# Convolution and two feed-forward layers on one core: early products issued singly, filler on TensorE, x split in thirds, a PSUM tile per bank

## The chip, the core and the metric

The kernel runs on one core of a Trainium2 chip. The time is the device time of one execution, in microseconds (us). A core has TensorE (PE; its weight loads are PEld), VectorE (DVE), ScalarE (ACT), GpSimd (POOL), and SyncE (SP), which issues the DMAs here. Every engine works through its own instructions in the order in which the program lists them.

## The reference

x is (2, 4096, 192), the convolution's weights (2, 4096, 8 heads, 7 taps); both layers have 2048 inner columns.

```python
w = softmax(weight_gen)                          # over the 7 taps
out = einsum('bshk,bskhg->bshg', w, x_unfolded)  # causal, 24 columns per head
x = out.reshape(8192, 192)
h = maximum(x @ w_in, 0.0);  y = h * h @ w_out                     # layer m=0
h = y @ w_in2;  z = (h * clip(h + 3, 0, 6) / 6) @ w_out2           # layer m=1
```

## The kernel before

The 8192 tokens are 16 blocks b of 512 columns. Each layer m takes a block in 8 steps, (m, b, f); a step covers two groups (FG) of 128 inner columns. All float32 operands of a product are split into a high and a low part in a reduced format, so a step has three sets of products: high by high, low weight by high, high by low.

A step has a part A (`make_A`, line 307: 18 matmuls of 64 rows into h, two at a time on the two halves of the array; group i uses rows 64i and up, so the 192 rows of x stand twice, once in each half) and a part B (`make_B`, line 318: the squared or gated h times w_out, into the sums `accs`, 128 rows and 64 rows). `emit_pair` (line 350) interleaves part A of one step with part B of the step three before (LAG = 3), the latter cut into 20 products of 64 rows; where there is no part A, as in the last three steps, part B is 10 products of 128 rows, first the six of the 128 rows (o = 0), then the four of the 64 rows (o = 1, line 361). Between A and B stand `relu` (ScalarE, line 386), `square` (ScalarE, 390) or `gate` (VectorE, 399), `high` (a cast, either engine, 406) and `low` (VectorE, 412). The tiles g, gh and gl have two buffers each.

The first two blocks (b < ON_PE = 2) have a start of their own. `convolve_pe` (line 671): VectorE multiplies one tap (`term`), TensorE adds it up in PSUM with an identity as weights (`total`, line 690: 4 matmuls of 64 rows per tap). `twice` (line 241) copies each third of the sums doubled into `x`, `turn_pe` (line 249) transposes it into `xt`, `split_pe_hi` (261) and `split_pe_lo` (266) split it, two thirds at once and then the last. Later blocks are convolved on VectorE alone (lines 642, 656) and transposed by VectorE and a round over DRAM; `split_hi` (228) and `split_lo` (234) split those. The sixteen steps of blocks 0 and 1 are woven, so that two steps in a row use one group of weights. The weights come as float64 words and are split by VectorE and ScalarE (lines 118 to 176), eight groups for each layer.

All operations are entered with a duration for each engine, what they depend on and which buffers they take; a list scheduler then plays them through and lists the instructions in the order of its start times. On each engine it takes, of what can start, the operation whose time limit is nearest. `finish_last` (line 471) brings out the last block: two evictions (488 on ScalarE, 490 on VectorE), eight small products (498, 499), two copies and two DMAs (504).

## Time and profile before

| | us |
|---|---|
| median of 3 runs | 1104.89 (1103.47 to 1105.0) |
| the profiled execution | 1104.57 |
| its span, first to last instruction | 1102.7 |
| TensorE busy | 1081.8 (98%) |
| VectorE busy | 929.1 (84%) |
| ScalarE busy | 597.4 (54%) |

Busy shares are means over the whole span. TensorE's matmuls are pipelined, so a busy TensorE is not yet at its peak, and its clock has two levels, 1.2 and 2.4 GHz; the page gives the granted clock as a share of the full one. What bounds a stretch is read from tables by stretch and from the chain of waits, which follows the work that ended last back to what released it.

### The profile page before, as it was taken

To read this page: it belongs to the slowest core of one execution; us is meant where nothing else is said; L and a number is where in the kernel's file an instruction comes from. 1 tells how busy PE (TensorE), PEld (TensorE's weight loads), DVE (VectorE), ACT (ScalarE), POOL (GpSimd) and SP (SyncE) were. 2 spreads that over 40 slices of the span, in tenths; PEclk is the share of its full clock that TensorE was granted. 3 is DMA by queue.
4 is the path that set the end of the run, shared out by engine and by line. 5 is a ranking of instruction groups with operands and counts; after the bars stand their busy time and mean duration, and the time that the engine had idled before them with its cause. 6 is when DMAs were issued, how large, how long until landed. Compare 5 with 4: busy or idle time off the path is not lost.

```text
span 1102.7 us, 23858 instructions
## 1 busy us (share of the span) xinstructions
PE 1081.8 (98%) x9846; PEld 934.3 (85%) x9846; DVE 929.1 (84%) x1018; ACT 597.4 (54%) x648; POOL 3.2 (0%) x11
## 2 busy tenths in 40 slices
PE   6899999999999999999999999999999999999998
PEld 3588888888888888888888888888888888888886
DVE  7799999999999999988787576676757888888875
ACT  3799999766645656363553536444353333333322
POOL 1000000000000000000000000000000000000000
PEclk9999999999999999999999999999999999999999
DMA  9702744043330622332221222212032222133101
GB/s 217 186 1 73 198 120 151 20 117 87 78 116 15 175 58 78 97 87 59 61 75 36 62 59 73 58 39 73 21 82 59 68 64 73 45 81 83 30 30 43
DMA packets 67509, 86.73 MB, mean 79 GB/s; under 512 B 5517, under 2 KB 43533, under 8 KB 66505
## 3 DMA queue, kind: packets, MB, share of 16 engines
q1 hardware_dynamic: 67256, 85.01, 29.3%
q8 instruction: 77, 1.26, 0.5%
q14 instruction: 32, 0.25, 0.1%
q10 hardware_dynamic: 144, 0.20, 0.0%
HBM read 59.10 MB, written 26.08 MB: 77 GB/s over the span
## 4 chain that ended last, share of the span: by engine, by line
PE 93%; DVE 3%; DMA 1%; ACT 1%; issue 1%; SPq 0%; DVEq 0%
PE acc L304 48%; PE h L304 44%; DMA st<-in_moe_w_in_dram 1%; PE acc L690 1%; DVE gl L412 1%; DVE a L656 0%; ACT g L386 0%; DMA xc<-in_x_dram 0%; ACT gh L406 0%; PE acc L361 0%; DVE g L399 0%; DVE sl L266 0%; DVE w L164 0%; SPq L90 0%; ACT x L247 0%
## 5 line engine op out<-in xcount | busy, mean ns | idle before, releaser
L304 PE MATMUL h<-sh,w 64*128 64x512 f32 x3072 | 524.6, 378 | 8.2 <-DVE sl L266 6.8
L304 PE MATMUL acc<-gh,w 64*128 64x512 f32 x3036 | 517.9, 376 | 0.0
L386 ACT ACTIVATE g<-h 128x1024 f32<-128x1024 f32 x256 | 262.2, 1024 | 469.4 <-PE h L304 448.2
L304 PEld LDWEIGHTS h<-sh,w 64*128 64x128 f32 x3072 | 383.3, 186 | 51.5 <-DVE sl L266 7.2
L304 PEld LDWEIGHTS acc<-gh,w 64*128 64x128 f32 x3036 | 379.8, 186 | 40.2
L304 PE MATMUL h<-sl,w 64*128 64x512 f32 x1536 | 358.7, 378 | 0.0
L304 PE MATMUL acc<-gl,w 64*128 64x512 f32 x2024 | 354.1, 376 | 0.0
L412 DVE TENSOR_TENSOR gl<-g,gh 128x1024 fp32r<-128x1024 f32 x256 | 312.3, 1220 | 15.9 <-ACT gh L406 11.3
L304 PEld LDWEIGHTS acc<-gl,w 64*128 64x128 f32 x2024 | 237.8, 186 | 26.8
L304 PEld LDWEIGHTS h<-sl,w 64*128 64x128 f32 x1536 | 238.7, 187 | 20.7
L399 DVE SCALAR_TENSOR_TENSOR g<-g,h 128x1024 f32<-128x1024 f32 x128 | 156.0, 1219 | 60.5 <-ACT g L386 59.7
L406 DVE CAST gh<-g 128x1024 fp32r<-128x1024 f32 x156 | 107.1, 686 | 44.9 <-PE acc L304 43.8
L390 ACT ACTIVATE g<-g 128x1024 f32<-128x1024 f32 x128 | 135.8, 1061 | 1.3
L406 ACT CAST gh<-g 128x1024 fp32r<-128x1024 f32 x100 | 104.4, 1044 | 4.2 <-PE acc L361 1.3
L642 DVE TENSOR_TENSOR pr<-xc,wc 128x768 f32<-128x768 f32 x84 | 79.8, 952 | 1.3 <-DMA xs<-aT 0.6
L656 DVE TENSOR_TENSOR a<-a,pr 128x768 f32<-128x768 f32 x84 | 79.7, 949 | 0.0
L234 DVE TENSOR_TENSOR sl<-x,sh 128x1536 fp32r<-128x1536 f32 x30 | 52.5, 1749 | 3.7 <-ACT sh L228 3.7
L424 DVE TENSOR_SCALAR z<-acc 128x512 f32<-128x512 f32 x30 | 20.7, 690 | 24.6 <-PE h L304 24.5
L228 ACT CAST sh<-x 128x1536 fp32r<-128x1536 f32 x27 | 39.8, 1474 | 1.6 <-DMA x<-xs 1.5
L690 PE MATMUL acc<-pp,ident 64*64 64x384 f32 x112 | 21.8, 548 | 6.6 <-DVE pp L681 6.6
L690 PEld LDWEIGHTS acc<-pp,ident 64*64 64x64 f32 x112 | 8.9, 152 | 18.5 <-issue 17.9
L128 ACT COPY t<-st 128x768 uint16<-128x768 uint16 x16 | 19.2, 1202 | 7.7 <-DMA st<-in_moe_w_out_dram 6.8
(54 smaller groups left out, 276.9 us busy)
## 6 DMA issues: line engine op xcount, KB each, us to landing
x<-ys SPq DMA_DIRECT2D x32, 512.0 KB, 6.2
x<-xs SPq DMA_DIRECT2D x28, 384.0 KB, 5.1
xc<-in_x_dram SPq DMA_DIRECT2D x7, 1344.0 KB, 7.5
ys<-z SPq DMA_DIRECT2D x32, 256.0 KB, 2.0
st<-in_moe_w_in_dram SPq DMA_DIRECT2D x32, 192.0 KB, 6.4
zq<-zs SPq DMA_DIRECT2D x60, 96.0 KB, 2.3
out_dram<-o SPq DMA_DIRECT2D x15, 384.0 KB, 2.3
xs<-aT SPq DMA_DIRECT2D x56, 96.0 KB, 2.9
```

The source lines that it names most:

```text
L228: copy_on(engine)(xs_in[m, b][0], xraw[m, b][:, 0:NK])
L234: nc.vector.tensor_tensor(out=lo, in0=src, in1=hi.bitcast(F32), op=ALU.subtract)
L304: return lambda: nc.tensor.matmul(ps, w[r], turns(x[r]), start=start, stop=stop)
L386: nc.scalar.activation(g, ps, AF.Relu, bias=3.0 if m else 0.0)
L390: nc.scalar.activation(g, g, AF.Square)
L399: nc.vector.scalar_tensor_tensor(out=g, in0=g, scalar=6.0, in1=h_ps[m, b, f], op0=ALU.min, op1=ALU.mult)
L406: copy_on(engine)(gh, g)
L412: nc.vector.tensor_tensor(out=gl, in0=g, in1=gh.bitcast(F32), op=ALU.subtract)
L424: nc.vector.tensor_scalar(out=dst, in0=src, scalar1=scale, scalar2=None, op0=ALU.mult)
L642: nc.vector.tensor_tensor(out=dst, in0=xs, in1=ws.to_broadcast([P, TB, H, G]), op=ALU.mult)
L656: nc.vector.tensor_tensor(out=total(), in0=total(), in1=prods.pop((b, k)), op=ALU.add)
L690: nc.tensor.matmul(attn[b][r, a, 0:2 * D], ident[r, r], v[r, a * 2 * D:(a + 1) * 2 * D], start=k == K - 1, stop=k == 0,)
```

## The change

Six things change. (1) For the first 16 steps part A and part B are separate operations: `products` is called once for A and, for the step's own part B, once more; part B alone is the form with 10 products of 128 rows. From step 16 on they are interleaved as before. (2) `spin` puts products identity x identity into PSUM columns that nobody reads, where the scheduler's TensorE has a gap of more than 0.8 us before 45 us; the first time it plans 4.2 us, then the gap less 0.4. (3) The sums have a PSUM tile for each bank (`acc_tiles`) instead of one for two banks; the taps are added by matmuls of 128 rows. (4) The first two blocks' x is copied once plus its first 64 columns (`copy_sums`), transposed in three overlapping windows, two of them into the sums' own tiles, and split third by third; in part A the second half of the array takes the thirds in another order (`by`). (5) The last step's part B begins with the 64 rows; `finish_last` evicts the 128 rows in two halves on two engines, and gh, gl of the step before the last get buffers of the split x. (6) The scheduler: a tap's sum is entered with 1.3 instead of 0.75 us, the first loads earlier, and an engine may hold back an operation for one that is more urgent by over GAIN = 6 us and would come before it ends less HOLD = 0.8. `relu` loses an argument and `relu_square`, which nothing called, goes; ON_PE is now TURNED.

```diff
-    def twice(b, j, engine):
-        if j == 0:
-            xraw[0, b] = x_tile()
-        d = xraw[0, b][:, j].rearrange("p (t h r) -> p t h r", t=TB, h=2)
-        src = attn[b][:, :, 0:2 * D].rearrange("p a (t d) -> p a t d", t=2)[:, :, :, j * HP:(j + 1) * HP]
-        for a in range(2):
-            copy_on(engine)(d[:, 2 * a:2 * a + 2], src[:, a].unsqueeze(2).to_broadcast([P, 2, 2, HP]))
+    xps, plain, spare, adding = {}, {}, [], []
+    def copy_sums(b, a, engine):
+        if a == 0:
+            plain[b] = x_tile().rearrange("p k n -> p (k n)")[:, 0:TB * (D + HP)].rearrange("p (t d) -> p t d", t=TB)
+        dst = plain[b][:, 2 * a:2 * a + 2]
+        src = attn[b][a][:, 0:2 * D].rearrange("p (t d) -> p t d", t=2)
+        copy_on(engine)(dst[:, :, 0:D], src)
+        copy_on(engine)(dst[:, :, D:], src[:, :, 0:HP])
 
     def turn_pe(b, j):
-        if j % 2 == 0:
-            xps[b, j] = ps_h.tile([P, 2, N], F32, tag="h", name="xt")
-        d = xraw[0, b][:, j].rearrange("p (t c) -> p t c", t=TB)
-        pv = xps[b, j // 2 * 2][:, j % 2].rearrange("d (q t r) -> d t q r", q=Q, t=TB)
+        if j < 2:
+            xps[b, j] = attn[b][j]
+        else:
+            room = ps_h.tile([P, 2, N], F32, tag="h", name="xt")
+            xps[b, j] = room[:, 0]
+            spare.append(room[:, 1, 0:P])
+        pv = xps[b, j].rearrange("d (q t r) -> d t q r", q=Q, t=TB)
         for t in range(TB):
-            nc.tensor.transpose(pv[:, t], d[:, t], ident)
+            nc.tensor.transpose(pv[:, t], plain[b][:, t, j * HP:j * HP + P], ident)
 
     def split_pe_hi(b, j, engine):
         if j == 0:
             xs_in[0, b] = [split_tile(n) for n in "hl"]
-        n = min(2, NK - j)
-        copy_on(engine)(xs_in[0, b][0][:, j:j + n], xps[b, j][:, 0:n])
+        copy_on(engine)(xs_in[0, b][0][:, j], xps[b, j])
 
     def split_pe_lo(b, j):
-        n = min(2, NK - j)
-        hi, lo = [v[:, j:j + n] for v in xs_in[0, b]]
-        nc.vector.tensor_tensor(out=lo, in0=xps[b, j][:, 0:n], in1=hi.bitcast(F32), op=ALU.subtract)
+        hi, lo = [v[:, j] for v in xs_in[0, b]]
+        nc.vector.tensor_tensor(out=lo, in0=xps[b, j], in1=hi.bitcast(F32), op=ALU.subtract)
...
     def make_A(m, b, f):
         w = [[w_in_of(m, f, h, j) for j in range(NK)] for h in range(2)]
-        x = [[v[:, j] for j in range(NK)] for v in xs_in[m, b]]
-        terms = [(w[h][j], x[l][j]) for h, l in ((0, 0), (1, 0), (0, 1)) for j in range(NK)]
+        x = xs_in[m, b]
+        terms = [(w[h][j], x[l], j) for h, l in ((0, 0), (1, 0), (0, 1)) for j in range(NK)]
         seqs = []
         ps = h_ps[m, b, f] = ps_h.tile([P, FG, N], F32, tag="h", name="h")
         for i in range(FG):
-            seqs.append([half(i, ps[:, i], w, x, n == 0, n == len(terms) - 1) for n, (w, x) in enumerate(terms)])
+            by = NK - 1 if i and m == 0 and b < TURNED else 0
+            seqs.append([
+                half(i, ps[:, i], w, x[:, (j + by) % NK], n == 0, n == len(terms) - 1)
+                for n, (w, x, j) in enumerate(terms)
+            ])
         return seqs
 
+    def acc_tiles():
+        return [ps_a.tile([P, N], F32, tag=f"acc{o}", name=f"acc{o}") for o in range(2)]
 
     def make_B(m, b, f):
         if f == 0:
-            acc = ps_a.tile([P, 2, N], F32, tag="acc", name="acc")
-            accs[m, b] = [acc[:, o] for o in range(2)]
+            accs[m, b] = acc_tiles()
         high, low = [[], []], [[], []]
         ghs, gls = g_sb.pop((m, b, f))
...
         if not A:
-            for ps, terms in zip(accs[m, b], N_R):
+            for o in (1, 0) if B == steps[-1] else (0, 1):
+                terms = N_R[o]
                 for n, (w, g) in enumerate(terms):
                     nc.tensor.matmul(
-                        ps, w, turns(g), start=(first and n == 0), stop=(last and n == len(terms) - 1)
+                        accs[m, b][o], w, turns(g), start=(first and n == 0), stop=(last and n == len(terms) - 1)
                     )
...
+    def part_tile(n, s):
+        if s == steps[-2]:
+            return act.tile([P, NK, N], F32R, tag=f"s{n}", name=f"g{n}", bufs=2)[:, 0:FG]
+        return gp.tile([P, FG, N], F32R, tag=f"g{n}", name=f"g{n}")
     def high(m, b, f, engine):
         g = g_sb[m, b, f]
-        gh = gp.tile([P, FG, N], F32R, tag="gh", name="gh")
+        gh = part_tile("h", (m, b, f))
         copy_on(engine)(gh, g)
         g_sb[m, b, f] = gh, g
 
     def low(m, b, f):
         gh, g = g_sb[m, b, f]
-        gl = gp.tile([P, FG, N], F32R, tag="gl", name="gl")
+        gl = part_tile("l", (m, b, f))
         nc.vector.tensor_tensor(out=gl, in0=g, in1=gh.bitcast(F32), op=ALU.subtract)
         g_sb[m, b, f] = gh, gl
...
     def finish_last(b):
         ov = o_v[:, b * TB:(b + 1) * TB, :].rearrange("(q r) t d -> r q t d", q=Q)
         acc = accs.pop((1, b))
-        spare = x_tile()
-        folds = spare[:, 0, 0:DR]
+        folds = x_tile()[:, 0, 0:DR]
         o = wtmp.tile([P, TB, D], F32, tag="q", name="o", bufs=2)
         for h in range(2):
             r = slice(h * DR, (h + 1) * DR)
             nc.gpsimd.tensor_copy(folds[r], ident[r, r])
-        zc = []
-        for i in (1, 0):
-            vv = spare[:, 1 + i]
-            v = vv.rearrange("d (t p) -> d t p", t=TB)
-            if i:
-                nc.scalar.activation(vv, acc[i], AF.Copy, scale=1.0 / 6.0)
-            else:
-                nc.vector.tensor_scalar(out=vv, in0=acc[i], scalar1=1.0 / 6.0, scalar2=None, op0=ALU.mult)
-            zc.append(v)
-        zr, zn = zc
+        zn, zr = [act.tile([P, N], F32, tag=f"z{i}", name=f"z{i}") for i in range(2)]
+        nc.scalar.activation(zr, acc[1], AF.Copy, scale=1.0 / 6.0)
+        c = [slice(i * N // 2, (i + 1) * N // 2) for i in range(2)]
+        nc.vector.tensor_scalar(out=zn[:, c[0]], in0=acc[0][:, c[0]], scalar1=1.0 / 6.0, scalar2=None, op0=ALU.mult)
+        nc.scalar.activation(zn[:, c[1]], acc[0][:, c[1]], AF.Copy, scale=1.0 / 6.0)
+        zn, zr = [v.rearrange("d (t p) -> d t p", t=TB) for v in (zn, zr)]
         for i in range(2):
             h = slice(2 * i, 2 * i + 2)
             ps = ps_h.tile([P, FG, N], F32, tag="h", name="ot")
             pv = ps[:, 0, 0:2 * D].rearrange("p (t d) -> p t d", t=2)
             for t in range(2):
                 nc.tensor.matmul(pv[:, t, P:D], zr[:, 2 * i + t], folds, start=True, stop=True)
+            for t in range(2):
...
     WEAVE = 1
-    ON_PE = 2
+    IDENT_AT, SPIN_UNTIL = 1.6, 45.0
+    APART = 16
+    HOLD = 0.8
+    GAIN = 6.0
     TAIL = {"PE": 0.2, "DVE": 0.09, "ACT": 0.1, "SP": 0.0}
...
+    def sums_tile(b):
+        if b not in attn:
+            attn[b] = acc_tiles()
+            spare.append(attn[b][0][:, N - P:N])
+    def spin(us):
+        if not spare:
+            sums_tile(0)
+        for _ in range(int(us / 0.22)):
+            nc.tensor.matmul(spare[-1], ident, ident, start=not adding, stop=not adding)
...
         def total(k):
-            if k == K - 1:
-                attn[b] = ps_a.tile([P, 2, N], F32, tag="acc", name="acc")
+            sums_tile(b)
+            adding[:] = [b] if k else []
             v = prods.pop((b, k)).rearrange("p t h g -> p (t h g)")
             for a in range(2):
-                for i in range(2):
-                    r = slice(i * HP, (i + 1) * HP)
-                    nc.tensor.matmul(
-                        attn[b][r, a, 0:2 * D], ident[r, r], v[r, a * 2 * D:(a + 1) * 2 * D],
-                        start=k == K - 1, stop=k == 0,
-                    )
+                nc.tensor.matmul(
+                    attn[b][a][:, 0:2 * D], ident, v[:, a * 2 * D:(a + 1) * 2 * D], start=k == K - 1, stop=k == 0
+                )
 
         o = t = None
...
-                {"PE": 0.75}, lambda k=k: total(k), [o] + ([t] if t else []), [acc] if k == K - 1 else [], [key, acc]
+                {"PE": 1.3}, lambda k=k: total(k), [o] + ([t] if t else []), [acc] if k == K - 1 else [], [key, acc]
...
-        dups = []
-        for j in range(NK):
-            t = {"ACT": 2 * act_t(N // 2), "DVE": 2 * (0.09 + 1.045e-3 * N / 2)}
-            dups.append(
-                add(t, lambda e, j=j: twice(b, j, e), deps + [(d, -99.0) for d in dups[:1]], [("x", (0, b))], [acc])
-            )
+        srcs, held = [], [("x", (0, b))]
+        t = {"ACT": act_t(2 * D) + act_t(P), "DVE": two(2 * D) + two(P)}
+        for a in range(2):
+            more = [(srcs[0], -99.0)] if a else []
+            srcs.append(add(t, lambda e, a=a: copy_sums(b, a, e), deps + more, held, [acc]))
         turns_pe, hi_pe, lo_pe = [], [], []
         for j in range(NK):
-            key = ("h", ("xt", b, j // 2 * 2))
-            t = {"PE": 1.0}
-            turns_pe.append(add(t, lambda j=j: turn_pe(b, j), [dups[j]] + turns_pe[-1:], [key], [("x", (0, b))]))
+            more = [(prev, -99.0)] if prev else []
+            takes = [("h", ("xt", b))] if j == 2 else []
+            turns_pe.append(
+                add({"PE": 0.62}, lambda j=j: turn_pe(b, j), srcs + turns_pe[-1:] + more, takes, held + [acc])
+            )
         splits = [("sh", (0, b)), ("sl", (0, b))]
-        for j in range(0, NK, 2):
-            key, cols = ("h", ("xt", b, j)), min(2, NK - j) * N
-            t = {"ACT": act_t(cols), "DVE": two(cols)}
-            deps = [turns_pe[min(j + 1, NK - 1)]] + hi_pe[-1:]
+        for j in range(NK):
+            key = ("h", ("xt", b)) if j == 2 else acc
             takes = splits if j == 0 else []
-            hi_pe.append(add(t, lambda e, j=j: split_pe_hi(b, j, e), deps, takes, [key] + splits))
-            t = {"DVE": two(cols)}
-            lo_pe.append(add(t, lambda j=j: split_pe_lo(b, j), hi_pe[-1:], uses=[key] + splits))
+            t = {"ACT": act_t(N), "DVE": two(N)}
+            hi_pe.append(
+                add(t, lambda e, j=j: split_pe_hi(b, j, e), turns_pe[j:j + 1] + hi_pe[:1], takes, [key] + splits)
+            )
+            lo_pe.append(add({"DVE": two(N)}, lambda j=j: split_pe_lo(b, j), hi_pe[-1:], uses=[key] + splits))
         x_ready[0, b], x_hi[0, b] = lo_pe, hi_pe
         prev = hi_pe[0]
         return turns_pe[-1]
...
+    def products(i, A, j, B):
+        deps, takes, uses = [], [], []
         if A:
             m, b, f = A
             if (m, b) not in x_ready:
                 prepare_x(m, b)
             k = (m, f // FG)
-            deps += [(hi, -0.0) for hi in x_hi[m, b]] + [(lo, -6 * SLOT) for lo in x_ready[m, b]]
-            deps += [hi_w[k], (lo_w[k], -3 * SLOT)]
+            deps += [(hi, -n * SLOT) for n, hi in enumerate(x_hi[m, b])]
+            deps += [(lo, -(6 + n) * SLOT) for n, lo in enumerate(x_ready[m, b])]
+            deps += [hi_w[k], (lo_w[k], -3 * SLOT), (before["A"], -1.0)]
             takes.append(("h", i))
             uses += [("sh", (m, b)), ("sl", (m, b))]
-        if Bs:
-            m, b, f = Bs
+        if B:
+            m, b, f = B
             k = (m, f // FG)
-            gh, gl = ready_g[i - LAG]
+            gh, gl = ready_g[j]
             early = (0.8, 1.6) if A else (0.0, 0.8)
-            deps += [hi_r[k], lo_r[k], (gh, -early[0]), (gl, -early[1])]
-            uses += [("gh", i - LAG), ("gl", i - LAG)]
+            deps += [hi_r[k], lo_r[k], (gh, -early[0]), (gl, -early[1]), (before["B"], -1.0)]
+            uses += part_keys(j)
             (takes if f == 0 else uses).append(("acc", (m, b)))
-        slots = (9 if A else 0) + (10 if Bs else 0)
-        p = prev_pe = add({"PE": slots * SLOT}, lambda A=A, Bs=Bs: emit_pair(A, Bs), deps, takes, uses)
-        due(p, at_step(i))
-        fixed[p] = at_step(i) + slots * SLOT
+        slots = (9 if A else 0) + (10 if B else 0)
+        p = add({"PE": slots * SLOT}, lambda: emit_pair(A, B), deps, takes, uses)
+        due(p, at_step(i if A else j + LAG))
+        fixed[p] = at_step(i if A else j + LAG) + slots * SLOT
         step_ops.append(p)
...
+    for i in range(NS + LAG):
+        A = steps[i] if i < NS else None
+        if i < APART:
+            products(i, A, None, None)
+            if i + LAG < APART:
+                products(None, None, i, A)
+        else:
+            products(i, A, i - LAG, steps[i - LAG])
 
     for o in ops:
         for d, lag in o.deps:
...
             if best is None:
+                continue
+            end = t + best.times[e] - HOLD
+            urgent = None
+            for o in pool:
+                if e in o.times and len(o.times) == 1 and o.limit + GAIN < best.limit:
+                    r = available(o, max(t, ready_at[o]))
+                    if t < r < end and (urgent is None or o.limit < urgent.limit):
+                        urgent = o
+                        soon = r
+            if urgent:
+                later = min(later, soon)
                 continue
             del pool[best]
...
+        idle = IDENT_AT
         for o in order:
+            if "PE" in o.times and idle < SPIN_UNTIL:
+                if o.start - idle > 0.8:
+                    spin(o.start - idle - 0.4 if idle > IDENT_AT else 4.2)
+                idle = o.start + o.times["PE"]
             emit(o, o.engine)
```

## Rows read from the trace of the kernel before

**Rows 1.** Stretches: busy us (instructions) of each engine, granted clock, DMA share, GB/s.
```profile
core 0: us, PE busy (x) PEld busy (x) DVE busy (x) ACT busy (x) POOL busy (x), PEclk, DMA share, GB/s
6.60:20.80 14.20, 13.70 (x68) 6.18 (x68) 9.41 (x16) 4.39 (x9) 0.00 (x0) 1.00 1.00 234
20.80:24.00 3.20, 0.00 (x0) 0.00 (x0) 3.20 (x8) 2.85 (x5) 0.00 (x0) 1.00 1.15 231
24.00:27.20 3.20, 3.15 (x20) 2.14 (x22) 3.20 (x5) 0.00 (x0) 0.00 (x0) 0.68 1.15 235
27.20:41.70 14.50, 13.98 (x87) 6.70 (x86) 11.50 (x17) 9.78 (x17) 0.00 (x0) 0.95 1.06 272
41.70:45.20 3.50, 0.03 (x2) 0.04 (x2) 2.45 (x3) 3.50 (x6) 0.00 (x0) 1.00 1.10 248
45.20:48.80 3.60, 3.60 (x20) 2.86 (x22) 3.60 (x8) 1.85 (x3) 0.00 (x0) 0.56 0.45 105
48.80:75.00 26.20, 26.20 (x244) 22.99 (x242) 24.04 (x33) 24.89 (x31) 0.00 (x0) 0.99 0.01 2
75.00:95.00 20.00, 18.95 (x174) 15.98 (x172) 20.00 (x27) 18.48 (x22) 0.00 (x0) 1.00 0.26 61
95.00:310.00 215.00, 215.00 (x1996) 188.61 (x1994) 209.81 (x245) 171.72 (x190) 0.00 (x0) 1.00 0.40 110
```

**Rows 2.** The chain of waits, 5 to 60 us: start, duration, what.
```profile
24.05 3.15 PE h L304 x18
27.20 6.00 PE acc L690 x32
```

**Rows 3.** Instructions in order of time, TensorE and its weight loads, the first sums.
```profile
6.61 11.66 PE L690 MATMUL acc<-pp,ident 64*64 64x384 f32 x56 [6.61 <-DVE pp L681]
...
7.28 0.26 PEld L690 LDWEIGHTS acc<-pp,ident 64*64 64x64 f32 x2 [0.38 <-issue]
...
12.29 0.15 PEld L690 LDWEIGHTS acc<-pp,ident 64*64 64x64 f32 x2 [0.17 <-issue]
```

**Rows 4.** Instructions in order of time, 1088 to 1093 us.
```profile
1088.59 0.69 DVE L406 CAST gh<-g 128x1024 fp32r<-128x1024 f32 x1 [0.22 <-PE acc L304]
1088.62 0.38 PE L304 MATMUL h<-sl,w 64*128 64x512 f32 x1
...
1088.92 1.13 PE L361 MATMUL acc<-gh,w 128*128 128x512 f32 x4
...
1092.53 0.70 PE L361 MATMUL acc<-gl,w 128*128 128x512 f32 x2 [0.32 <-DVE gl L412]
```

**Rows 5.** The chain of waits, last part.
```profile
1096.28 0.61 ACT x L488
...
1096.91 0.70 DVE x L490
...
1098.88 0.48 ACT o L503
```

**Rows 6.** Instructions in order of time, GpSimd, 0 to 7 us.
```profile
1.06 0.29 POOL masks.py:199 TENSOR_SCALAR_AFFINE_SELECT ident<-ident 128x128 f32<-128x128 f32 x1
```

**Rows 7.** Instructions in order of time, VectorE, 2 to 24 us.
```profile
11.86 0.96 DVE L681 TENSOR_TENSOR pp<-xc,wc 128x768 f32<-128x768 f32 x1 [2.69 <-PE acc L690]
...
19.54 0.76 DVE L247 COPY x<-acc 128x256 f32<-128x256 f32 x2 [2.09 <-ACT x L247]
```

**Rows 8.** Instructions in order of time: a lower third, the transposes, a third's cast.
```profile
24.78 0.68 DVE L266 TENSOR_TENSOR sl<-xt,sh 128x512 fp32r<-128x512 f32 x1
...
39.84 1.82 PE L255 MATMUL xt<-ident,x 128*128 128x128 f32 x12 [0.47 <-ACT x L247]
...
44.22 0.63 ACT L261 CAST sh<-xt 128x512 fp32r<-128x512 f32 x1
```

**Rows 9.** Groups by line, VectorE, 95 to 310 us: count, busy us, mean ns.
```profile
L412 DVE TENSOR_TENSOR gl<-g,gh 128x1024 fp32r<-128x1024 f32 x52 | 63.3, 1218 | 2.0 <-ACT gh L406 1.2
...
L234 DVE TENSOR_TENSOR sl<-x,sh 128x1536 fp32r<-128x1536 f32 x8 | 13.9, 1742 | 0.0
L406 DVE CAST gh<-g 128x1024 fp32r<-128x1024 f32 x15 | 10.2, 678 | 0.0
```

63 lines of the change are left out of this document (32 added, 31 removed).

## The prediction

> **What bounds the kernel now.** I read the table of stretches first [rows 1]. From 95 us to 310 us TensorE (PE) is busy in all 215 us, and the page's forty slices show it full up to the last one: there only less work would help, and the change takes none away. 1996 matmuls fill those 215 us, 0.1077 us each, so a step's products into h (18) cost 1.94 us and its products into the sums (20) 2.15 us. What can still move lies ahead of 95 us and in the last 20.
>
> Ahead of 95 us TensorE loses time in two ways. It waits: 3.2 us in 20.8-24.0, 3.5 us in 41.7-45.2, 1.05 us in 75-95 [rows 1], and some 1.2 us around the two sets of transposes. And it runs slowly after each wait: the granted clock is 0.68 of full in 24.0-27.2 and 0.56 in 45.2-48.8 [rows 1], so at the lower of its two levels (1.2 of 2.4 GHz) for much of them. The chain of waits shows the price [rows 2]: the first 18 products take 3.15 us where 1.94 would do (1.2 lost), the 32 sums behind them 6.00 where 16 pairs of 0.32 are 5.1 (0.9 lost). The step from 45.2 takes 3.6 for 1.94 (1.65 lost) [rows 1]. The very first sums show it in the weight loads [rows 3]: a pair of them comes every 0.26 + 0.38 = 0.64 us at 7 us and every 0.15 + 0.17 = 0.32 at 12 us. The 56 matmuls, 28 pairs, take 11.66 us where 28 x 0.32 = 9.0 would do (2.7 lost). Together 3.2 + 3.5 + 1.05 + 1.2 + 1.2 + 0.9 + 1.65 + 2.7 = 15.4 us.
>
> Then the same table for VectorE (DVE). It is busy 24.04 of 26.2 us in 48.8-75 and all 20 us in 75-95 [rows 1]. So TensorE's waits are not the whole story: the sixteen woven steps need all eight weight groups of the first layer, and VectorE prepares them. ScalarE is as full there (24.89 of 26.2, 18.48 of 20).
>
> Last the tail: a stall of 0.32 us for gl [rows 4], and behind the last matmul (1096.26) a chain in single file, ScalarE 0.61, VectorE 0.70, transposes up to 1098.88 [rows 5].
>
> **The change, part by part.**
>
> *Filler on TensorE.* The planner puts identity x identity products into gaps before 45 us. The first is int(4.2/0.22) = 19 of them. A pass of 384 columns costs 0.64 at the lower clock [rows 3], so 128 columns cost 0.21 and the two passes of one product 0.43 (an estimate from those rows). All 19 slow: 8.1 us; about half of them fast: 6 us. They start when the identity is written, about 1.4 us [rows 6], so they end between 7.5 and 9.6; I take 8.1, since in 6.6-11.6 the clock rose some 5 us after TensorE began. The first sums are ready at 6.6, so the filler costs them 1.5 us and gives back 2.7: they end at 8.1 + 9.0 = 17.1 instead of 18.3. The new form (two products of 128 rows and 384 columns per tap instead of four on quarters) has four passes of 0.32, no cheaper: 1.28 us per tap both ways. VectorE's fifth tap, which waits 2.69 us for TensorE [rows 7], starts at 8.1 + 2 x 1.28 = 10.7 instead of 11.86.
>
> *x in thirds, fewer copies.* Two copies of 384 and two of 128 columns replace six doubled ones; the upper half of third j now holds third j+1. The copies of the two halves can run side by side: about 0.65 us, bounded by 1.3 if one waits for the other, as in [rows 7] VectorE's copy waits 2.09 us on ScalarE's. Twelve transposes take 1.82 us [rows 8], a third of them 0.6. Then three casts of 512 columns, 0.63 each [rows 8]. The reordered terms make the first pair of products of step 0 read third 0 and third 2, so it waits for all three casts, and pipelining saves less than it seems: 17.1 + 0.65 + 0.6 + 1.9 + 0.1 = 20.3. Filler between transposes and step 0 writes the tile that the third cast reads; if that orders the two, up to 0.9 us of filler comes behind the cast. I take 0.3: step 0 starts at 20.6 (before 24.05 [rows 2]) and, at full clock, ends at 22.6 instead of 27.2. **4.6 us ahead.**
>
> *Products issued singly.* Step i's products into h and step i-3's into the sums become two operations for i < 16, the latter as ten products of 128 rows, so 10 x 0.2155 = 2.15 us as before. Sums of step 0 no longer stand behind step 3's products: they can fill the second hole, 41.7-45.2. TensorE's work in 27.2-41.7 is nearly gapless, 13.98 us of 14.5, of which 1.82 are transposes [rows 1, 8]; less those and the 0.9 of slow clock it is 11.3 us and ends at 22.6 + 11.3 = 33.9. Copies, transposes and casts as above plus 1 us of ScalarE's other work: step 2 starts at 38.1 (45.17), ends at 40.1 (48.8), and 2.15 us of sums are already done: 8.7 + 2.15 = **10.9 us ahead for TensorE alone.** Its cost: some 26 switches between 64-row and 128-row products. The last one of before shows 0.30 us between starts (1088.62 to 1088.92 [rows 4]), 0.09 more than a normal slot of 0.2155; 26 x 0.09 = 2.3 at most, 0 where TensorE waits for VectorE anyway. I take 0 and keep 2.3 in the range.
>
> *The cap.* VectorE's work up to 95 us does not shrink (three splits of 0.68 [rows 8] for 1.21 + 0.68, some copies more). It can only be moved into its idle time. What lies before 6.6 waits for loads and stays. After that it is 4.79 (6.6-20.8), 3.0 (27.2-41.7), 1.05 (41.7-45.2) and 2.16 (48.8-75) [rows 1]: 11.0 us. What ended it were TensorE at the slow clock and ScalarE's order [rows 7], both touched here: taps planned at 1.3 instead of 0.75 us put ScalarE's copies where they belong. I take 70%: **7.7 us**; ends 4 (only the first waits) and 11 (all).
>
> *After 95 us.* The lead stays only if VectorE keeps step. In 95-310 it has 5.2 us idle, and 15 casts of 0.68 = 10.2 us [rows 9] that ScalarE (171.7 of 215) could take. Nothing is added there but another order, from the new rule that an engine may hold back for a more urgent operation. I put it at 0. The m=1 steps' code is the same.
>
> *The tail.* gl of step 254 stands behind a cast that waited for a free buffer and came at 1088.59 [rows 4]; with buffers of its own (those of the split x, long free) the stall goes. From 1088.92 TensorE has 14 products before it needs gl, to 1088.92 + 14 x 0.2155 = 1091.94, and went on at 1092.53; less the 0.1 that it also loses at a switch, 0.5 us. The last step's 64 rows first: ScalarE's 0.6 us lies beside six matmuls (1.3 us), provided that the two sums are tiles of their own. Then the 128 rows in halves: VectorE 0.40, ScalarE 0.33 (0.70 and 0.61 for whole ones [rows 5]), two last transposes 0.33, hops 0.1. In the trace of before VectorE starts 0.02 us behind ScalarE's end though the two read different halves of the sums [rows 5], so readers of one sum's tile go one after the other: 0.40 + 0.33 + 0.33 + 0.1 = 1.16, against 1098.88 - 1096.26 = 2.62. Gain 1.46 + 0.5 = 1.96; bounds 0.9 (ScalarE's part stays behind the last matmul) and 2.3 (halves side by side). I take **1.8**.
>
> The Trainium skill, "PSUM — Partial Sum Buffer", section on bank collisions, speaks against the split eviction: no two engines may read one bank's partitions at once, even in other columns, so they have to be ordered. The trace agrees with ordering, and shows it even across two banks of one tile. By that rule the halves cost 0.73 in single file, without it 0.40, and the end would come 0.33 earlier.
>
> **The sum.** The profiled execution took 1104.57 us with a span of 1102.7. 1104.57 - 7.7 - 1.8 = 1095.1; the median of the three runs is 0.3 above the profiled one, so **1095.4 us**. With the bounds 4 to 11 and 0.9 to 2.3: 1091.6 to 1100.0 (0.9 + 4 and 2.3 + 11 off 1104.9).
>
> **Rivals.**
> 1. *VectorE and ScalarE give it back.* TensorE arrives early at 60-95 us and waits there for weights; only the tail and 1 to 3 us are left: 1100 to 1102. For it: VectorE at 20 of 20 and ScalarE at 18.48 of 20 in 75-95 [rows 1]. Against: 11 us of idle before, with causes that the change touches. Chance 0.16.
> 2. *Slower: the new hold-back idles VectorE.* It may wait for up to the operation's planned length less 0.8: 0.36 us per gl, 0.89 per split, about 0.09 per convolution product or sum. In 95-310 there are 52 gl and 8 splits [rows 9]: 18.7 + 7.1 = 26 us if every one were held, the shorter operations aside. VectorE can bear 5.2 + 10.2 = 15.4; above that TensorE stalls, and above 15.4 + 9.5 = 25 the kernel is slower. With all of these and 4 us of the shorter ones held: 1095.4 + 30 - 15.4 = 1110. Against: it asks for an operation 6 us more urgent, which few pairs can show. Chance 0.09.
> 3. *The filler does not do what it says:* it delays what it fills for and the clock is no higher at step 0. Then the start loses 1.5 + 0.9, keeps 2.15 of early sums and some of VectorE's better order (2 us), and the tail: 1104.9 - 1.8 - 1.8 = 1101.3, same to slightly faster. Chance 0.07.
> 4. *More than forecast:* conv 3's products, 2 us of VectorE's work in 86-92, also give way, and all idle goes: 1089 to 1091.5. Chance 0.06.
>
> **How the numbers follow.** Forecast 0.62 (1091.6 to 1100.0), rivals 0.16, 0.09, 0.07, 0.06. For 8 in 10 the range adds rivals 1 and 3 and a little below: 1090.5 to 1102.5, leaving out the slower case and part of the ends. A measurement of this kernel can tell about 0.2% (2.2 us, 1102.7) from no change. Faster: 0.62 + 0.13 + 0.05 + 0.06 = 0.86, less some for what none of these names: 0.82. Same 0.08, slower 0.10.
>
> **What would show it.** First sums end near 17, step 0 starts near 20.6 and step 2 near 38; clock 1.0 in both; sums of step 0 before step 2's products; VectorE's idle time between 6.6 and 95 down from 11 to 3-4 us; no 0.32 stall at the end, and some 1.2 us from the last matmul of the sums to the last copy instead of 2.6. Wrong if VectorE idles as long as before ahead of 95 us, or if TensorE shows gaps after 95 us.

## The result and the profile after

The changed kernel takes **1094.58 us** (median of four runs, 1094.28 to 1095.16) against 1104.18 (1103.34 to 1105.0) for the kernel before on the same chip: a ratio of 0.9914, 95% interval 0.9897 to 0.9931. The profiled execution took 1094.45 us with a span of 1092.7. Forecast were 1095.4 us, of it 7.7 at the start and 1.8 in the tail.

One instruction splits the gain in two: the first product of the last three steps, from which on TensorE has only 128-row products and the end. Before it came at 1088.92 [rows 4] with 13.78 us to the end of the span; after it comes at 1080.38 with 12.32 to go. So **8.54 us** came from what lies ahead and **1.46** from the tail.

The table of stretches of the changed kernel, columns as in [rows 1] (length; then busy us of PE, PEld, DVE, ACT, POOL; granted clock, DMA share, GB/s):

```profile
6.60:20.80 14.20, 13.08 (x60) 8.93 (x59) 12.05 (x23) 6.37 (x12) 0.00 (x0) 1.00 0.99 238
20.80:24.00 3.20, 3.20 (x20) 2.43 (x19) 3.20 (x5) 2.11 (x4) 0.00 (x0) 1.00 1.16 262
24.00:27.20 3.20, 3.20 (x17) 1.95 (x17) 3.20 (x5) 0.44 (x2) 0.00 (x0) 1.00 1.12 263
27.20:41.70 14.50, 14.50 (x80) 10.31 (x78) 14.04 (x23) 13.58 (x20) 0.00 (x0) 1.00 1.10 291
41.70:45.20 3.50, 3.50 (x34) 3.08 (x36) 3.50 (x6) 2.24 (x5) 0.00 (x0) 1.00 0.99 200
45.20:48.80 3.60, 3.54 (x34) 2.79 (x32) 3.60 (x9) 3.60 (x5) 0.00 (x0) 1.00 0.04 12
48.80:75.00 26.20, 26.20 (x166) 20.68 (x163) 25.96 (x34) 25.47 (x30) 0.00 (x0) 1.00 0.00 1
75.00:95.00 20.00, 20.00 (x134) 16.01 (x133) 18.81 (x23) 18.39 (x22) 0.00 (x0) 1.00 0.27 60
```

The clock is 1.00 where it was 0.68 and 0.56, the two holes of TensorE are closed, and so are the 1.05 us lost in 75-95. VectorE's idle time between 6.6 and 95 us fell from 11.0 us [rows 1] to 4.0.

TensorE's instructions in order of time show what filled the holes (start, us, engine, line, operation, tiles, count, idle time before it):

```profile
1.40 7.36 PE L686 MATMUL acc<-ident 128*128 128x128 f32 x38 [1.40 <-POOL ident masks.py:199]
8.60 9.21 PE L705 MATMUL acc<-pp,ident 128*128 128x384 f32 x28
18.93 2.05 PE L686 MATMUL acc<-ident 128*128 128x128 f32 x16 [1.12 <-ACT x L248]
...
26.09 1.56 PE L306 MATMUL h<-sh,w 64*128 64x512 f32 x12
...
33.15 2.85 PE L705 MATMUL acc<-pp,ident 128*128 128x384 f32 x8
35.54 1.32 PE L370 MATMUL acc<-gh,w 128*128 128x512 f32 x4
...
37.99 1.04 PE L259 MATMUL acc<-ident,x 128*128 128x128 f32 x8
...
41.56 1.56 PE L306 MATMUL h<-sh,w 64*128 64x512 f32 x12
...
43.61 1.46 PE L306 MATMUL h<-sh,w 64*128 64x512 f32 x12
```

L686 is filler (two records for each product), L705 the sums of the convolution's taps (four for each tap), L259 the transposes of x, L306 the products into h, L370 the sums issued singly. Step 0 begins at 26.09, two us *later* than before [rows 2], because three of the next block's taps and 2 us of filler now stand ahead of it. Step 2 begins at 41.56 and step 3 follows at 43.61, and two steps' sums (L370, twice 2.15 us) are done by then. Before, step 3 began at 48.73 with no sum done.

That gives TensorE's ledger: at step 3 it is 48.73 - 43.61 + 2 x 2.15 = 9.4 us ahead. From there to step 16, the first that both kernels issue in a pair with sums, it gains what the kernel before lost and pays for the switches between 64-row and 128-row products. One round of them in the change, and the start of step 16:

```profile
60.81 1.56 PE L306 MATMUL h<-sh,w 64*128 64x512 f32 x12
...
62.95 1.13 PE L370 MATMUL acc<-gh,w 128*128 128x512 f32 x4
...
65.30 1.56 PE L306 MATMUL h<-sh,w 64*128 64x512 f32 x12
...
95.98 1.34 PE L306 MATMUL h<-sh,w 64*128 64x512 f32 x9
```

Step 16 in the kernel before:

```profile
103.80 1.24 PE L304 MATMUL h<-sh,w 64*128 64x512 f32 x9
```

From 60.81 to 62.95 are 2.14 us for 18 products that need 1.94, and from 62.95 to 65.30 are 2.35 for ten that need 2.15: 0.40 us for a round, 3.2 for the eight between 48 and 96 us. Another 0.2 goes at a short wait at 47.7. The kernel before loses 1.8 in the same steps (55.07 us from 48.73 to 103.80 for 13 pairs of 4.10), most of it at the waits in 85-96, of which [rows 1] shows 1.05 as idle. 9.4 + 1.8 - 3.4 = 7.8, which is 103.80 - 95.98. The last switch takes 0.1, so the start is worth **7.7 us**. The lead then grows to 8.54 between 310 and 450 us, where the kernel before waits again (0.34 us idle, and what the products around it lose) and the change does not.

The tail of the changed kernel, in order of time:

```profile
1085.97 0.60 ACT L490 ACTIVATE z<-acc 128x512 f32<-128x512 f32 x1 [2.10 <-PE acc L370]
...
1087.22 0.42 DVE L492 TENSOR_SCALAR z<-acc 128x256 f32<-128x256 f32 x1 [2.09 <-PE acc L370]
1087.68 0.38 ACT L493 ACTIVATE z<-acc 128x256 f32<-128x256 f32 x1 [1.11 <-DVE z L492]
...
1087.97 0.56 PE L500 MATMUL ot<-x,z 128*128 128x64 f32 x4
...
1088.37 0.39 PE L502 MATMUL ot<-ident,z 128*128 128x128 f32 x2
...
1088.79 0.48 ACT L506 COPY o<-ot 128x384 f32<-128x384 f32 x1 [0.73 <-PE ot L502]
```

The 64 rows' z (L490) lies beside the products, as planned. From the last sum to the last copy are 1087.20 to 1088.79, 1.59 us instead of 2.62.

### The profile page after: what moved, and what is told of

It reads as the page before. It is cut to its first block, busy times and chain, and to the rows that moved or that the text cites. A ratio compares the mean times of both kernels' runs of the same rounds, so it can differ in the third digit from the quotient of the medians.

```text
span 1092.7 us, 23517 instructions
## 1 busy us (share of the span) xinstructions
PE 1086.0 (99%) x9714; PEld 938.5 (86%) x9714; DVE 932.3 (85%) x1020; ACT 593.9 (54%) x647; POOL 3.5 (0%) x11
## 3 DMA queue, kind: packets, MB, share of 16 engines
q8 instruction: 76, 1.25, 0.5%
## 4 chain that ended last, share of the span: by engine, by line
PE 97%; DMA 1%; ACT 1%; DVE 1%; SPq 1%; issue 0%; ACTq 0%
PE acc L306 47%; PE h L306 45%; PE acc L370 3%; PE acc L705 1%; DMA st<-in_moe_w_out_dram 1%; DMA xc<-in_x_dram 0%; SPq L91 0%; DVE hb L143 0%; ACT t L129 0%; PE acc L686 0%; ACT g L395 0%; DVE sl L268 0%; SPq L97 0%; ACT g L399 0%; ACT gh L415 0%
## 5 line engine op out<-in xcount | busy, mean ns | idle before, releaser
L306 PE MATMUL h<-sh,w 64*128 64x512 f32 x3072 | 515.9, 377 | 0.1
L306 PE MATMUL acc<-gh,w 64*128 64x512 f32 x2880 | 491.3, 376 | 0.0
L306 PEld LDWEIGHTS h<-sh,w 64*128 64x128 f32 x3072 | 376.8, 186 | 45.7 <-issue 1.9
L306 PEld LDWEIGHTS acc<-gh,w 64*128 64x128 f32 x2880 | 359.6, 186 | 39.3
L306 PE MATMUL h<-sl,w 64*128 64x512 f32 x1536 | 349.5, 376 | 0.0
L306 PE MATMUL acc<-gl,w 64*128 64x512 f32 x1920 | 335.9, 376 | 0.0
L421 DVE TENSOR_TENSOR gl<-g,gh 128x1024 fp32r<-128x1024 f32 x256 | 312.0, 1219 | 19.2 <-ACT gh L415 13.1
L306 PEld LDWEIGHTS h<-sl,w 64*128 64x128 f32 x1536 | 232.9, 186 | 20.9
L306 PEld LDWEIGHTS acc<-gl,w 64*128 64x128 f32 x1920 | 225.0, 186 | 26.2
L229 ACT CAST sh<-x 128x1536 fp32r<-128x1536 f32 x22 | 32.4, 1471 | 0.1
L370 PE MATMUL acc<-gh,w 128*128 128x512 f32 x96 | 27.3, 393 | 0.0
L129 ACT COPY t<-st 128x768 uint16<-128x768 uint16 x16 | 18.9, 1184 | 8.2 <-DMA st<-in_moe_w_out_dram 8.2
L370 PEld LDWEIGHTS acc<-gh,w 128*128 128x128 f32 x96 | 17.3, 189 | 5.2 <-issue 2.0
```

What stands on the lines that cost most here:

```text
L129: nc.scalar.copy(wtile("t", m, g)[:, :, 0], quarters(wst[m, g])[:, :, 1])
L229: copy_on(engine)(xs_in[m, b][0], xraw[m, b][:, 0:NK])
L306: return lambda: nc.tensor.matmul(ps, w[r], turns(x[r]), start=start, stop=stop)
L370: nc.tensor.matmul(accs[m, b][o], w, turns(g), start=(first and n == 0), stop=(last and n == len(terms) - 1))
L421: nc.vector.tensor_tensor(out=gl, in0=g, in1=gh.bitcast(F32), op=ALU.subtract)
```

## The experiments

No kernel leaves work out. "Tail starts" is the first product of the last three steps in the trace; the ratio is to the kernel before as measured beside it, whose medians lay between 1104.18 and 1104.88, so differences of less than some 0.7 us say nothing.

| kernel | median us | ratio, 95% interval | tail starts |
|---|---|---|---|
| before | 1104.18 | 1 | 1088.9 |
| the change | 1094.58 | 0.9914 (0.9897-0.9931) | 1080.4 |
| e1 no filler | 1095.24 | 0.9917 (0.9902-0.9931) | 1080.3 |
| e2 first filler only | 1094.72 | 0.9913 (0.9899-0.9928) | 1080.8 |
| e3 paired steps | 1099.71 | 0.9957 (0.9943-0.9971) | 1086.3 |
| e4 no hold-back | 1101.85 | 0.9973 (0.9963-0.9983) | 1087.3 |
| e5 single to step 8 | 1094.21 | 0.9908 (0.9890-0.9926) | 1079.7 |
| e6 paired, no filler | 1095.46 | 0.9919 (0.9903-0.9935) | 1081.3 |
| e7 no hold-back, no filler | 1098.65 | 0.9947 (0.9932-0.9963) | 1084.7 |
| e8 before + hold-back | 1103.34 | 0.9991 (0.9981-1.0001) | 1086.9 |
| e9 tap's sum planned at 0.75, no filler | 1094.95 | 0.9916 (0.9901-0.9931) | 1080.8 |
| e10 thirds 0 and 1 together, no filler | 1095.56 | 0.9917 (0.9902-0.9932) | 1081.5 |
| e11 before + hold-back + tap at 1.3 | 1100.68 | 0.9963 (0.9950-0.9975) | 1085.5 |
| e12 64-row products first, single to 8, no filler | 1093.61 | 0.9900 (0.9885-0.9915) | 1080.4 |

My theory was the prediction's: TensorE's holes are filled, and VectorE's idle time ahead of 95 us caps what that is worth. The rival was that TensorE's filler and single issue add little and that the order of the plan makes the gain. The first four runs take the parts away one by one. The totals of e2, e4, e9, e10, e11 and e12 fell into the range of one of the theories written down ahead of them, that of e8 at the edge of one; those of e1, e5, e6 and e7 lay between or beside the ranges, and e3 hit theory C's range for another reason than theory C's.

### The filler: e1 and e2

```diff
-    IDENT_AT, SPIN_UNTIL = 1.6, 45.0
+    IDENT_AT, SPIN_UNTIL = 1.6, 0.0
```

That is e1; e2 sets 1.7 instead of 0.0, so that only the filler ahead of the first sums stays.

> The changed kernel without any identity products on TensorE; all other instructions stand in the same order on every engine. Theory A (the filler pays for itself at most: what it warms it delays): the first sums start at 6.7 instead of 8.6 us, run in pairs of 0.64 us until the clock rises and end near 18.3 instead of 17.8; the transposes then follow the copies directly, near 19.3 instead of 20.85; total 1093.3 to 1094.3. Theory B (the filler is what holds the clock up): granted clock 0.6 to 0.7 at step 0 and again later, total 1096.5 to 1098.

> Only the first 19 identity products are kept; the 8 that the changed kernel issues between the copies of the sums and the transposes (18.93 to 20.98 us) go. Theory A (from there to 95 us TensorE is the bound, so every product in its queue costs its time): the transposes start at 18.95, total 1 to 2 us less, 1092.6 to 1093.6. Theory B (VectorE's supply is the cap): TensorE waits for VectorE later by as much, total 1094.3 to 1094.9.

Neither can be told from the change (1095.24 and 1094.72 against 1094.58). TensorE without any filler, in order of time:

```profile
6.67 10.84 PE L705 MATMUL acc<-pp,ident 128*128 128x384 f32 x28 [6.67 <-DVE pp L698]
...
40.84 1.64 PE L306 MATMUL h<-sh,w 64*128 64x512 f32 x12
...
47.66 1.56 PE L306 MATMUL h<-sh,w 64*128 64x512 f32 x12 [0.65 <-ACT g L395]
```

The first sums start 1.9 us earlier and run slower (10.84 us instead of 9.21), so they end at 17.5 against 17.8: what the warm clock gave back, the filler had taken. Step 0 starts 1.1 us earlier (24.95), step 2 0.7. Then TensorE waits 0.65 us and goes on at 47.66, where with filler it went on at 47.72. The chain of waits of the changed kernel names what it meets there:

```profile
43.94 1.11 DVE hb L143
...
45.07 0.72 ACT w L152
45.79 0.96 ACT g L399
46.75 0.92 ACT g L395
...
47.72 2.21 PE h L306 x18
```

VectorE prepares a weight group (hb), ScalarE casts it and then works off g in its own order. A TensorE that comes earlier than 47.7 waits for these two (0.65 us in e1; in e2 0.60, up to 48.10). So the cap of the prediction is real in e1, with ScalarE in it as well as VectorE; in the change itself ScalarE's g ends at 47.67, and TensorE's next products start 0.05 us later.

Whether filler keeps the clock up behind the first sums, these runs do not settle. Without filler at that place, e1, e2 and e9 show a granted clock of 1.00 in 20.8-24.0, but e6, e7, e10 and e12 show 0.50 to 0.56; with it, the change, e4 and e5 show 1.00 and e3 0.72. e1 and e6 wait there almost equally long for the copies (1.57 and 1.64 us), and only e6 runs at the lower of the two levels behind the wait:

```profile
20.80:24.00 3.20, 3.18 (x7) 1.86 (x8) 2.67 (x4) 1.98 (x3) 0.00 (x0) 0.50 1.16 224
```

Its step 0 starts at 26.98, the change's at 26.09 behind 2 us of filler, e1's at 24.95, and the three totals lie within 0.9 us.

### Products in pairs: e3, e6 and e5

```diff
-    APART = 16
+    APART = 3
```

That is e3. e6 also sets SPIN_UNTIL to 0.0; e5 keeps the filler and sets APART to 8.

> All else of the change, but steps 3 to 15 interleaved in pairs as before (only the first three steps' products into h stand alone). Theory A (single issue fills the hole ahead of step 2 with two steps' sums, 4.3 us, and pays about 2.3 us for switching between 64-row and 128-row products): 2 to 3 us slower, 1096.5 to 1097.5, a hole of 3 to 4 us before step 2. Theory B (the switches cost as much as the hole): 1094 to 1095. Theory C (single issue is most of the gain, since it also frees the buffers of g earlier for VectorE): 5 us or more slower, 1099.5 or more.

e3 costs 5.1 us, and reading it alone would credit them to the single issue. Its trace at the second hole, on TensorE in order of time, says otherwise:

```profile
43.38 3.30 PE L686 MATMUL xt<-ident 128*128 128x128 f32 x14 [3.25 <-DVE sl L268]
46.62 1.56 PE L306 MATMUL h<-sh,w 64*128 64x512 f32 x12
```

Without single sums the hole stays, the planner puts filler in it, and the filler fills nothing: it writes the tile that VectorE's split (L268) still reads, waits 3.25 us for it, and then runs 3.30 us (14 records, 7 products) in front of step 2. So pairs were tried again without filler:

> Steps 3 to 15 in pairs as in e3, and no filler at all. In e3 the filler ahead of step 2 stood behind VectorE's split (it writes the tile that the split reads) and ran 3.3 us at the lower clock after it. Theory A (half of what e3 lost is that filler, the rest the hole): step 2 starts near 42.2 us instead of 46.7, at a granted clock of 0.6, total 1096.2 to 1097.3. Theory B (the hole alone costs the 5 us; the filler hides in it): 1099.2 to 1100.2.

e6 is 4.25 us faster than e3 and only 0.2 slower than e1 (no measurable difference), and faster than both theories. In its trace the hole is there, but in pieces:

```profile
37.83 1.09 PE L259 MATMUL acc<-ident,x 128*128 128x128 f32 x8 [0.94 <-ACT x L248]
...
39.99 0.48 PE L306 MATMUL h<-sh,w 64*128 64x512 f32 x1 [0.63 <-ACT sh L264]
...
41.70 1.56 PE L306 MATMUL h<-sh,w 64*128 64x512 f32 x11 [1.23 <-ACT sh L264]
```

TensorE waits 0.94 + 0.63 + 1.23 = 2.8 us, starts most of step 2 when the change does (41.70, 41.56), and has no sums done then. It pays no switches later, and its VectorE is busy 46.12 of 46.2 us in 48.8-95. What single issue gains early (4.3 us of sums) it loses for the larger part to switches (3.2); the tails of e6 and e1 start 1.0 us apart.

> Only the first 8 steps are issued singly; steps 8 to 15 are interleaved in pairs as before. In the changed kernel each pair of switches between 64-row and 128-row products leaves gaps of 0.19 and 0.10 us, eight times between 49 and 96 us. Theory A (TensorE is the bound there): four or five of the eight go, 1.2 to 1.5 us less, 1093.1 to 1093.5. Theory B (VectorE and ScalarE cap that stretch): 1094.3 to 1095, with TensorE waiting for them by as much.

With fewer switches 0.4 us are gained at most, inside the spread of the runs, though a round of them costs 0.40 us and not the 0.29 of this expectation. The table of stretches of e5 shows the reason:

```profile
48.80:75.00 26.20, 26.20 (x208) 21.95 (x208) 26.09 (x37) 25.91 (x30) 0.00 (x0) 1.00 0.00 1
75.00:95.00 20.00, 19.53 (x182) 16.82 (x180) 19.83 (x24) 18.14 (x21) 0.00 (x0) 1.00 0.28 61
```

VectorE is busy 26.09 + 19.83 = 45.9 of 46.2 us, and TensorE, earlier by the saved switches, waits 0.5 us for its gl (L421), the only wait that the trace lists for it in 50-1085.

### The hold-back: e4, e7 and e8

The rule lets an engine leave a ready operation for one that is 6 us more urgent and ready before the first would end.

```diff
-    GAIN = 6.0
+    GAIN = 1e9
```

That is e4; e7 also sets SPIN_UNTIL to 0.0. The rule holds for VectorE and ScalarE as well as for TensorE.

> The scheduler's holding back is switched off (it would need an operation more urgent by a billion us); all else is as in the changed kernel. Theory A (it changes little): within 0.5 us of 1094.6, VectorE's idle time in 6.6 to 95 us near 4 us. Theory B (it is what keeps the engines' orders right in the crowded stretch): 2 us or more slower, with TensorE waiting in 20 to 95 us.

> Holding back off as in e4, and no filler at all. In e4 step 2 came behind a wait of 2.3 us for VectorE's split and 1.2 us of filler. Theory A (the order of VectorE's work is the loss): 1 to 2 us less than e4, 1099.8 to 1100.9, so 5 us or more of holding back's worth remain. Theory B (holding back only keeps the filler from standing in the way): 1095 to 1097.

Without the rule the change keeps only 3 of its 9.6 us (e4); without rule and filler it loses 3.4 us against e1 (e7). This was the largest single effect that I found, and the prediction had put it at 0. e4 shows the damage by the filler again: 3.2 us of its 7.3 go with it, and it stands in the same place:

```profile
43.96 1.16 PE L686 MATMUL xt<-ident 128*128 128x128 f32 x8 [2.29 <-DVE sl L268]
```

The rest is seen in e7, on TensorE in order of time, with VectorE's product of the next block's last tap (L698) at its place:

```profile
30.96 0.96 DVE L698 TENSOR_TENSOR pp<-xc,wc 128x768 f32<-128x768 f32 x1 [0.74 <-PE acc L705]
...
35.38 1.32 PE L370 MATMUL acc<-gh,w 128*128 128x512 f32 x4
...
37.83 1.45 PE L705 MATMUL acc<-pp,ident 128*128 128x384 f32 x4
...
41.28 1.04 PE L259 MATMUL acc<-ident,x 128*128 128x128 f32 x8
...
43.67 1.56 PE L306 MATMUL h<-sh,w 64*128 64x512 f32 x11 [0.48 <-ACT sh L264]
```

In the change the last two taps' sums of the next block (L705, x8) run at 33.15 and then step 0's sums (L370). In e7 the plan takes the sums of step 0 first, and the last tap's (x4) stands behind them, at 37.83, though its product was done at 31.92, ahead of step 0's gl (34.56). So it is TensorE's order that holds it up, not VectorE. On it hang copies, transposes, casts and splits of that block: the transposes come at 41.28 instead of 37.99, step 2 at 43.67 instead of 40.84 in e1. That is 2.8 us; a wait of 1.03 us for a cast of x (sh, L229) at 165 us, which the table of waits lists, makes 3.8, against 3.4 between the medians and 4.35 between the two profiled executions. What the rule does here shows in **TensorE's** queue. I had looked for its price on VectorE. No run switches it off for one engine alone, so how much of the 3.4 is TensorE's order is read from the traces.

```diff
+    HOLD = 0.8
+    GAIN = 6.0
...
+            end = t + best.times[e] - HOLD
+            urgent = None
+            for o in pool:
+                if e in o.times and len(o.times) == 1 and o.limit + GAIN < best.limit:
+                    r = available(o, max(t, ready_at[o]))
...
+            if urgent:
+                later = min(later, soon)
...
```

> The kernel before with the one new rule of the scheduler (hold back for an operation more urgent by over 6 us that would come before the other ends less 0.8 us); no single issue, no filler, no other tiles. Theory A (the rule is worth as much here, since it orders VectorE's work in the crowded start): 1098 to 1100.5. Theory B (it is worth something only where TensorE has other work to fill the hole): within 1.5 us of 1104.9.

The rule alone in the kernel before brings 1.1 us, within what can be told from no change: both holes are still there, and nothing else is at hand to fill them:

```profile
23.18 2.82 PE L304 MATMUL h<-sh,w 64*128 64x512 f32 x12 [3.26 <-DVE sl L266]
...
44.35 2.93 PE L304 MATMUL h<-sh,w 64*128 64x512 f32 x12 [3.51 <-DVE sl L266]
```

### The planned length of a tap's sum: e11 and e9

```diff
-                {"PE": 0.75}, lambda k=k: total(k), ...
+                {"PE": 1.3}, lambda k=k: total(k), ...
```

e11 is the kernel before with the hold-back and this line.

> The kernel before with two edits of the scheduler's numbers alone: holding back as in e8, and 1.3 instead of 0.75 us for a tap's sum. TensorE's list then has sums of the second block ahead of step 0. Theory A (order alone brings a good part): the wait of 3.3 us ahead of step 0 goes, its clock stays up, the one ahead of step 2 stays; 1100 to 1101.5. Theory B (without thirds and tiles for each bank the holes only move): as e8, 1102.8 to 1103.9.

Two edits of the plan, with no instruction changed, give 3.9 us. In order of time on TensorE:

```profile
19.64 1.51 PE L255 MATMUL xt<-ident,x 128*128 128x128 f32 x8 [2.01 <-ACT x L247]
...
25.86 1.56 PE L304 MATMUL h<-sh,w 64*128 64x512 f32 x12
...
44.12 2.79 PE L304 MATMUL h<-sh,w 64*128 64x512 f32 x12 [4.12 <-DVE sl L266]
```

With a tap's sum planned at what it takes, the planner puts two taps of the next block ahead of step 0, and the wait of 3.3 us right ahead of it is gone; a shorter one, 2.01 us for the copies ahead of the transposes, stands in its place, with a granted clock of 0.53 in 20.8-24.0. The second hole (4.12 us, then a clock below full) remains. Of the change's 9.6 us, 3.9 are this and 1.5 the tail; some 4.2 are left (5.1 by where the tails start), mostly about the second hole. They need the rest of the change: its own tiles, plain copies, thirds and single issue. Undoing only single issue (e6) or only the split of the first two thirds costs under 1 us:

```diff
-        for j in range(NK):
+        parts = ((0, 1), (2,))
+        for js in parts:
```

So in e10, without filler, transposes, casts and splits go in two groups.

> The changed kernel without filler (as e1), the first two blocks' x transposed, cast and split as two thirds together and then the last, as before, instead of third by third; the copies, tiles and instructions are those of the change. Theory A (thirds shorten the way from the sums to step 2): step 2 starts 1 to 2 us later than in e1, total 1096.2 to 1097.2. Theory B (VectorE's work is the same and caps the stretch to 48 us): 1094.9 to 1095.8.

Step 2 starts at 42.63, 1.8 us later than in e1, as theory A has it, but the total is 0.3 us from e1, no difference that can be told. Undoing both at once was not tried, nor were the tiles or the copies, so how the 4.2 us divide among these parts stays open.

> The changed kernel without filler (as e1), a tap's sum entered in the scheduler with 0.75 us on TensorE as before instead of 1.3. TensorE's list then has step 0 ahead of all sums of the second block, as the kernel before had. Theory A (the right duration is what fills the hole ahead of step 0): a wait of 2 to 3 us ahead of step 0 and 2 to 3 us more than e1, 1097 to 1098.5. Theory B (the later cap by VectorE hides it): 1094.9 to 1095.9.

e9 is the converse of e11, in the change without filler: the tap's sum planned at 0.75. The waits at step 0 come back, but the time does not change (1094.95, e1 1095.24):

```profile
20.13 0.48 PE L306 MATMUL h<-sh,w 64*128 64x512 f32 x1 [0.45 <-ACT sh L264]
22.02 1.56 PE L306 MATMUL h<-sh,w 64*128 64x512 f32 x11 [1.41 <-ACT sh L264]
```

Step 0 starts 3 to 5 us earlier than in e1 (its first product at 20.13, the others at 22.02), and step 2 1.1 us later (41.90). What TensorE does not do ahead of step 0 it does behind it. The start of step 0, on which the prediction spent most of its working, decides nothing here, and the planned length that is worth 2.7 us in the kernel before (e8 to e11) is worth nothing in the change.

### A faster tail: e12

```diff
-                nc.tensor.matmul(pv[:, t, P:D], zr[:, 2 * i + t], folds, start=True, stop=True)
...
+        for i in range(2):
...
+            for t in range(2):
+                nc.tensor.matmul(pvs[i][:, t, P:D], zr[:, 2 * i + t], folds, start=True, stop=True)
```

All four 64-row products stand ahead of the transposes.

> The changed kernel without filler, with single issue for 8 steps, and at the very end all four products of the 64 rows ahead of the transposes of the 128 rows (in the changed kernel two of the four stand behind the first two transposes, 0.39 us). From the last matmul of the sums to the last copy 1.25 to 1.35 us instead of 1.59; total 1093.3 to 1094.2. Rival: ScalarE's half of the eviction then ends the wait, 1.5 us; total 1094.0 to 1094.8.

With single issue to step 8 and no filler it has the lowest median, 1093.61 us, but its interval overlaps the change's. The chain of waits at its end:

```profile
1087.24 0.84 PE ot L500 x8
1088.08 0.55 PE ot L505 x4
...
1088.65 0.48 ACT o L509
```

From the last sum to the last copy are 1.41 us instead of 1.59, between the 1.25 to 1.35 expected and the rival's 1.5. All of it is now TensorE's work in one file: 12 records of 8 products, 1.39 us.

## Why the prediction was right in its total, and where its steps failed

**Right: the size of the cap.** The prediction took 70% of VectorE's 11.0 idle us [rows 1]; the trace shows 11.0 - 4.0 = 7.0 recovered, 63%, and 7.7 us for TensorE up to step 16 (forecast 7.7). That the two agree so well is luck in part: the 70% was chosen between bounds of 4 and 11, and TensorE's own terms, which make the 7.7, were all sized otherwise. The 0.8 us that came after 310 us were put at nothing. The mechanism holds only in part. In the change TensorE has no gap of 0.1 us between 18.9 us and the tail, so there its own work sets the end (9.4 us ahead where 10.9 were forecast, and 3.2 for switches where 0 was taken). VectorE and ScalarE set it as soon as TensorE gets some tenths of a microsecond earlier: TensorE waits 0.65 us in e1, 0.5 in e5. That the time hardly moves in e1, e2, e5, e6, e9 and e10 agrees with two limits that lie within about 1 us of each other. VectorE's own work was never varied, so this is read from waits and busy times and is not shown by a run that moves the cap.

**Wrong: the hold-back at 0, or as the second rival.** The prediction looked for what it could cost VectorE in 95-310 and found "few pairs". What it changed is seen at 28-38 us on TensorE, and in the changed kernel it was worth 3.4 us (e7) to 7.3 (e4). "Nothing is added there but another order" was the sentence that should have been worked out, for the stretch ahead of 95 us too: a good part of the holes came of the order of TensorE's queue ahead of 45 us. The forecast reached nearly the right total all the same, because it took the order that the rule makes for granted when it let VectorE's work move into its idle time.

**Wrong: the filler.** It was to end the first sums at 17.1 (17.8; 17.5 without it) and to keep the clock up. The clock is 1.00, but e1 has that without it; at step 2 (41.7-45.2) it is 1.00 in all six runs without filler, and only ahead of step 0 (20.8-24.0) do four of these fall to 0.50 to 0.56. The third rival ("delays what it fills for") was right about the filler and wrong about the sum, which it tied to it: in e3 and e4 it costs 4.3 and 3.2 us, in the change nothing that can be told, for there no hole is left ahead of step 2 for it to stand in.

**Wrong: step 0 at 20.6.** It starts at 26.09. The working followed one block's chain and left out that the planner would put three of the next block's taps (L705) and 8 filler products (16 records) in front. e9 shows that this costs nothing by itself. Step 2 was forecast at 38.1 with one step's sums done; it came at 41.56 with two. 3.5 us later and 2.15 us more done: 9.4 instead of 10.9 ahead.

**Mis-sized: the switches.** Bounded at 2.3 us (26 x 0.09) and taken as 0 "where TensorE waits for VectorE anyway". Between 48 and 96 us 16 of them cost 3.2 us, 0.2 each, and TensorE did not wait there. The row that the prediction read shows only what is lost ahead of a switch; the first products behind it lose as much again. But with fewer of them VectorE takes the place (e5), so 0 for the total was near.

**The tail: 1.46 for 1.8.** The stall of the first part went as forecast: from the first of its products to the last sum are 1080.38 to 1087.20, 6.8 us instead of 7.3, so 0.5. Of the chain behind the last sum 1.46 was forecast and 1.03 came; 0.1 of that is lost again behind the last copy. The mis-sized term was 1.16 for halves and transposes, with nothing else in TensorE's queue. The 64-row products of the second half (four records, 0.39 us in the chain) stand between the first and the last transposes; the row of L500 at 1087.97 is theirs. e12 takes them out of that place, and gets 0.18 of the 0.43 back.

The rule of the Trainium skill ("PSUM — Partial Sum Buffer", bank collisions) was followed in the trace: ScalarE's half, which waits for VectorE's, starts at 1087.68, 0.04 us after VectorE's (1087.22 + 0.42) ends. The 0.33 us that the prediction hung on it do not show, for TensorE is busy with other products until 1088.37 and ScalarE's half is done at 1088.06.

## What to carry to other kernels

When a list planner orders several engines, read a hole as a question of who stands in front: compare the order of the queue of the *idle* engine, and give the planner the measured length of each operation, before adding work to fill the hole (here that was worth 2.7 us in the kernel before and nothing once the other parts were in). A part undone beside a harmful part looks larger than it is (single issue: 5.1 us with the filler, 0.2 without), so undo parts in pairs before crediting one. And once two engines' limits lie within 1 us of each other, as they seem to here, edits to either alone stop paying; then only the tail, or less work on both, is left.

## What the runs showed of the hardware that I had not expected

A filler product whose output tile still has a reader is no filler: it waits for that reader (3.25 us in e3, 2.29 in e4), after which the step that it was to warm up stands behind it for another 3.3 or 1.2 us. The granted clock was 0.70 of full in 41.7-45.2 of e3 all the same.

A change between products of 64 rows and products of 128 rows cost about 0.2 us either way, 0.40 for a round (60.81 to 65.30: 4.49 us for 28 products that need 4.09), where the prediction had read 0.09 from one row. The Trainium skill ("TensorEngine Tiling (Array Packing)", section "Key Properties") says that a change of the tiling mode drains TensorE; the trace agrees in that every change costs time, and gives the price.
